# Weight halves and sums laid out in DRAM in parts of 2,048 bytes a partition

## The chip, the cores and the metric

The kernel runs on one core of one Trainium2 chip. The metric is device time in microseconds (us), from the start of the program to its end. All times below are of the whole program, and the trace is of one profiled execution.

## The reference

Eight batches of attention with a softmax over the feature axis of q and over the sequence axis of k, then a gated feed-forward network over all 4,608 tokens:

```
q_s = softmax(q, last axis); k_s = softmax(k, sequence axis)
kv  = einsum('bhsd,bhse->bhde', k_s, v)            # 8 batches, 8 heads, 576 x 64
x   = einsum('bhsd,bhde->bhse', q_s, kv)  -> (4608, 512)
xn  = x / sqrt(mean(x*x) + 1e-6) * rms_g
out = (silu(xn @ w_gate) * (xn @ w_val)) @ w_out   # 512 -> 1536 -> 512
```

All inputs and outputs are float32.

## The kernel before

The 4,608 tokens are nine blocks of 512. Each float32 product is made of three TensorE products of a high and a low half (`float32r`), so every weight is held as a pair of halves. The first three blocks run plainly: `f1` multiplies the normalised tokens by a tile of gate and value weights, `f2` multiplies the gated result by a tile of output weights; a step number s counts 12 tiles per block. The other six blocks are three pairs. A pair goes through a Strassen scheme: seven products (`pp`, numbered 1 to 7) of sums of weight quarters with sums of token blocks take the place of eight, for each of six tile pairs i and two column groups m. The last two pairs do the same for the output weights (`qq`).

The halves are made once, in block 1 (`w_hi`, `w_lo`, `o_hi`, `o_lo`), and kept in DRAM: `w_keep` (line 940) writes the four parts of a weight tile, `s_keep` (line 981) the sums of weights that the Strassen products need, `o_keep` (line 944) the halves of the output weights. They go to tensors `wd` (one for each of six tile pairs) and `od` (one for each of 12 tiles). These writes are issued from SyncE (SP). They are read back from GpSimd's queue (POOL): `w_back` (line 948) and `o_back` (line 952) for block 2, `w_in` (line 1118) and `o_in` (line 1130) for the pairs. A `w_in` brings part 1 (four parts: S2, S1, A11, A12; 1,024 KB) or part 2 (three parts: A22, S3, S4; 768 KB) of one m into a slot of a ring; there are four slots, and a slot is loaded again right behind the last product that reads it.

An explicit list, `ORDER`, gives the order in which the steps are written, and so the order on each engine and each queue; a letter behind a step (A, D, P) names the engine for it. POOL also computes: it makes low halves (`h_lo`, line 1017; `hp_lo`, line 1220), token sums (`t_add`, line 1089) and parts of the softmax of q. Between the plain blocks and the pairs, at about 340 to 380 us, block 2's last tiles, the first token sums of pair 0 and the attention of blocks 5 and 6 stand side by side. `q_load` (line 670) brings a q tile from DRAM in pieces of 128-byte runs through SP's queue; `q_max` (line 736) on VectorE (DVE) is the first to read it.

The layout before, and the reads and writes that use it, are these lines:

```
wd = [tc.dram_tile([2, P, 8, 2, HALF], F32, ...)]       # m, partition, part, half, 256
od = [tc.dram_tile([P, 2, DM], F32, ...)]
parts_of(i, at, n): wd[i][:, :, at:at + n] -> "m p a b f -> p m a (b f)"
w_in: src = wd[i][m, :, :4] if part == 1 else wd[i][m, :, 5:]     # one run a partition
```

Of the kernel before, what the change touches and what calls it, by code (L numbers as in the profile page):

```python
# [8 lines left out]
F32 = mybir.dt.float32  # L9
I32 = mybir.dt.int32  # L10
U32 = mybir.dt.uint32
F32R = mybir.dt.float32r
# [337 lines left out]
def linear_attention_then_gated_ffn(ctx: ExitStack, tc, q, k, v, w_gate, w_val, w_out, rms_g, out):  # L350
    nc = tc.nc
    B, H, S, D = q.shape
    NT, DM = out.shape
    DF = w_gate.shape[1]
    P = 128
    NG = H // 2
    NKT = DM // P
    NF = DF // P
# [14 lines left out]
    NH = NF // 2  # L373
    HALF = TB // 2
    assert NB == JP + 2 * NPAIR and NKT == 4 and NF == 2 * NH

    wsp = ctx.enter_context(tc.tile_pool(name="wsp", bufs=2))
# [28 lines left out]
    def on(default):  # L406
        return unit[0] or default
# [488 lines left out]
    wh_, wo_, h_, po, g_, v_ = {}, {}, {}, {}, {}, {}  # L896
    ov = out.rearrange("(j t p) m -> j t p m", p=P, t=T)
    ov0 = out.rearrange("(j p t) m -> j t p m", p=P, t=T)

    def w_tile(s):  # L900
        if s not in wh_:
            wh_[s] = wsp.tile([P, 2, 2, 2, HALF], F32R, name="w")
        return wh_[s]

    def o_tile(s):
# [9 lines left out]
    def w_hi(s, a, n):  # L915
        copy(w_tile(s)[:, a:a + n, :, 0], halves(s % NF, a, n), nc.scalar)

    def w_lo(s, a):
        w = w_tile(s)[:, a]
        on(nc.gpsimd).tensor_tensor(out=w[:, :, 1], in0=halves(s % NF, a, 1)[:, 0], in1=w[:, :, 0].bitcast(F32),  # L920
                                    op=ALU.subtract)
# [6 lines left out]
        on(nc.vector).tensor_tensor(out=ol, in0=W(s % NF, 2), in1=oh.bitcast(F32), op=ALU.subtract)  # L928

    S2, S1, A11, A12, A21, A22, S3, S4 = range(8)  # L930
    wd = [tc.dram_tile([2, P, 8, 2, HALF], F32, name=f"wd{i}") for i in range(NH)]
    od = [tc.dram_tile([P, 2, DM], F32, name=f"od{i}") for i in range(NF)]
    ot_ = {}

    def parts_of(i, at, n):
        return wd[i][:, :, at:at + n].rearrange("m p a b f -> p m a (b f)")

    def w_keep(s):
        i, odd = divmod(s % NF, 2)
        on(nc.sync).dma_start(parts_of(i, A21 if odd else A11, 2),  # L940
                          wh_[s].rearrange("p m a b f -> p m a (b f)").bitcast(F32))

    def o_keep(s):
        on(nc.sync).dma_start(od[s % NF], ot_[s].bitcast(F32))

    def w_back(s):
        i, odd = divmod(s % NF, 2)
        nc.gpsimd.dma_start(w_tile(s).rearrange("p m a b f -> p m a (b f)"), parts_of(i, A21 if odd else A11, 2))

    def o_back(s):  # L950
        o = wsp.tile([P, 2, DM], F32R, name="o")
# [26 lines left out]
        on(nc.gpsimd).tensor_tensor(out=t[:, :, 1], in0=f, in1=t[:, :, 0].bitcast(F32), op=ALU.subtract)  # L978

    def s_keep(i, n):  # L980
        on(nc.sync).dma_start(parts_of(i, {1: S1, 2: S2, 3: S3, 4: S4}[n], 1)[:, :, 0],
                          split[i, n].rearrange("p m b f -> p m (b f)").bitcast(F32))

    done = {}
# [57 lines left out]
    XF, XO, RING, WO, H2, TMP, HH = {}, {}, {}, [], {}, {}, {}  # L1042
# [61 lines left out]
    def ring():  # L1104
        if not RING:
            t0 = big.tile([P, 6, TB], F32R, name="ring_0", tag="raw_0")
            t1 = big.tile([P, 6, TB], F32R, name="ring_1", tag="raw_1")
            RING[1] = [t0[:, :4]]
            RING[2] = [t1[:, :3], t1[:, 3:]]
            WO.append(t0[:, 4:])  # L1110

    def w_in(p, i, m, part):
        ring()
        if part == 1 and m == len(RING[1]):
            RING[1].append(wsp.tile([P, 4, TB], F32R, name="w"))
        t = RING[part][m].rearrange("p a b -> p (a b)")
        src = wd[i][m, :, :4] if part == 1 else wd[i][m, :, 5:]
        nc.gpsimd.dma_start(t, src.rearrange("p a b f -> p (a b f)"))  # L1118

    def o_in(p, t, c):  # L1120
        ring()
# [309 lines left out]
    def e_put(x, h):  # L1431
# [7 lines left out]
              n_t, n_y0, n_y1, o_hi, o_lo, q_c0, q_eps0, q_exp, q_half, q_half2, q_hi, q_lo, q_load, q_load0, q_max,  # L1439
              q_max0, q_max2, q_mul, q_mul0, q_rec, q_rec0, q_sub, q_sub0, q_sum, q_sum0, q_sum2, q_t, q_t0, q_x, q_x0,  # L1440
              silu, store, w_keep, o_keep, w_back, o_back, s_add, s_hi, s_lo, s_keep, x_cp, x_nm, t_add, b_hi, b_lo,
              w_in, o_in, r_keep, r_load, t_sum, t_hi, t_lo, t_keep, qw, q_t1, q_t2, q_t3, q_t4, qb_hi, qb_lo, qq, qs1, qu2, qu3,
              q22, q21, q12, qtr, qput, qpua, pp, c_s1, c_u2, c_u3, c_11, c_21, c_22, c_12, gate, hm, e_add, e_tr, e_copy, e_put, hp_hi, hp_lo, f2p, put, v_load, v_ones, w_hi, w_lo, warm, x_acc, x_hi, x_lo, x_sq)}

# [33 lines left out]
```

## Time and profile before

| what | value |
|---|---|
| runs | 943.98, 944.52, 946.81 us |
| median | 944.52 us |
| profiled execution, its own time | 944.05 us |
| its span, first to last instruction | 941.8 us |
| TensorE (PE) busy | 924.7 us, 98% of the span |
| PE weight loads busy | 748.9 us |
| VectorE (DVE) busy | 729.5 us, 77% |
| ScalarE (ACT) busy | 467.4 us, 50% |
| GpSimd (POOL) busy | 532.8 us, 57% |
| DMA packets, all queues | 210,298 for 212.65 MB |
| POOL's DMA queue (q0) | 16,320 packets, 88.09 MB |
| SP's DMA queue (q1) | 187,568 packets, 122.86 MB |

An engine's busy time divided by the span is its share; PE's is near the whole, so its idle times, and what ended them, are what there is to win. "PE" rows are matmuls, "PEld" rows the loads of the stationary operand. The two DMA queues share 16 DMA engines; a packet of the trace is one run of bytes.

### The profile page before, as it was taken

To read this page: it belongs to the slowest core of one execution; us is meant where nothing else is said; L and a number is where in the kernel's file an instruction comes from. 1 tells how busy PE (TensorE), PEld (TensorE's weight loads), DVE (VectorE), ACT (ScalarE), POOL (GpSimd) and SP (SyncE) were. 2 spreads that over 40 slices of the span, in tenths; PEclk is the share of its full clock that TensorE was granted. 3 is DMA by queue.
4 is the path that set the end of the run, shared out by engine and by line. 5 is a ranking of instruction groups with operands and counts; after the bars stand their busy time and mean duration, and the time that the engine had idled before them with its cause. 6 is when DMAs were issued, how large, how long until landed. Compare 5 with 4: busy or idle time off the path is not lost.

```text
span 941.8 us, 14336 instructions
## 1 busy us (share of the span) xinstructions
PE 924.7 (98%) x4621; PEld 748.9 (80%) x4621; DVE 729.5 (77%) x1526; ACT 467.4 (50%) x748; POOL 532.8 (57%) x546
## 2 busy tenths in 40 slices
PE   8999999999999998999999999999999999999998
PEld 6687877887877886888888888888888888888886
DVE  6989879988978996877877788775458975646586
ACT  4998848765678764655644364322215522111241
POOL 4887978877677995667764535433532423332403
PEclk9999999999999999999999999999999999999999
DMA  9997528989977999798995699888665778855255
GB/s 237 285 249 227 157 47 283 295 269 311 289 247 210 240 249 239 192 254 223 254 248 181 198 286 282 279 292 296 187 210 176 218 193 264 271 203 179 66 158 90
DMA packets 210298, 212.65 MB, mean 226 GB/s; under 512 B 132144, under 2 KB 171568, under 8 KB 205616
## 3 DMA queue, kind: packets, MB, share of 16 engines
q1 hardware_dynamic: 187568, 122.86, 47.7%
q0 software_dynamic: 16320, 88.09, 29.9%
q10 hardware_dynamic: 6336, 0.79, 0.6%
q8 instruction: 37, 0.61, 0.3%
q14 instruction: 37, 0.30, 0.1%
HBM read 161.35 MB, written 50.33 MB: 225 GB/s over the span
## 4 chain that ended last, share of the span: by engine, by line
PE 83%; DMA 7%; DVE 3%; ACT 2%; issue 2%; SPq 2%; POOL 0%; DVEq 0%; ACTq 0%
PE ps_gv L1145 18%; PE ps_gv L996 14%; PE ps_o L1145 12%; PE ps_o L1033 7%; PE ps_a L1145 7%; PE ps_o L1354 6%; PE ps_o L1238 4%; PE ps_a L1354 4%; PE ps_gv L1354 3%; DMA qt<-in_q_dram 2%; PE ps_a L1238 2%; PE ps_gv L1238 2%; DMA w<-in_v_dram 2%; PE ps_a L600 2%; PE ps_a L808 2%
## 5 line engine op out<-in xcount | busy, mean ns | idle before, releaser
L996 PE MATMUL ps_gv<-xh,w 128*128 128x512 f32 x576 | 191.8, 399 | 1.1 <-DVE gs L1008 1.1
L1145 PE MATMUL ps_gv<-x,ring 128*128 128x512 f32 x576 | 143.0, 392 | 0.0
L996 PEld LDWEIGHTS ps_gv<-xh,w 128*128 128x128 f32 x576 | 108.5, 188 | 26.9 <-DVE gs L1008 2.1
L1145 PEld LDWEIGHTS ps_gv<-x,ring 128*128 128x128 f32 x576 | 107.0, 188 | 23.0
L996 PE MATMUL ps_gv<-xl,w 128*128 128x512 f32 x288 | 112.6, 392 | 0.0
L1166 DVE TENSOR_TENSOR tmp<-tmp,ps_gv 128x512 f32<-128x512 f32 x84 | 57.3, 684 | 49.5 <-PE ps_gv L1145 47.8
L1145 PE MATMUL ps_o<-x,ring 128*128 128x512 f32 x360 | 85.1, 389 | 0.0
L1118 POOL DMA_DIRECT2D ring<-wd x54 | 31.0, 575 | 91.2 <-PE ps_o L1145 34.1
L1145 PEld LDWEIGHTS ps_o<-x,ring 128*128 128x128 f32 x360 | 67.6, 188 | 14.2
L1033 PE MATMUL ps_o<-o,hh 128*128 128x512 f32 x288 | 73.5, 396 | 0.0
L996 PEld LDWEIGHTS ps_gv<-xl,w 128*128 128x128 f32 x288 | 54.5, 189 | 10.7 <-issue 0.4
L1033 PEld LDWEIGHTS ps_o<-o,hh 128*128 128x128 f32 x288 | 52.9, 188 | 11.8 <-ACT ot L416 0.7
L1166 DVE TENSOR_TENSOR tmp<-tmp,ps_o 128x512 f32<-128x512 f32 x42 | 28.7, 685 | 29.1 <-PE ps_o L1145 25.7
L920 POOL TENSOR_TENSOR w<-w,w 128x512 fp32r<-128x512 f32 x34 | 45.9, 1359 | 8.2 <-ACT w L411 7.6
L411 ACT CAST hh<-gs 128x512 fp32r<-128x512 f32 x48 | 29.6, 617 | 30.4 <-DVE gs L1008 16.0
L1033 PE MATMUL ps_o<-o,hl 128*128 128x512 f32 x144 | 39.7, 399 | 4.3 <-DVE hl L1017 4.3
L1118 POOL DMA_DIRECT2D w<-wd x18 | 10.1, 559 | 58.0 <-PE ps_a L1145 37.8
L547 DVE TENSOR_REDUCE cm<-kt 128x128 f32<-128x640 f32 x28 | 36.7, 1312 | 3.1 <-DMA kt<-in_k_dram 3.0
L1145 PE MATMUL ps_a<-x,w 128*128 128x512 f32 x144 | 36.9, 392 | 0.0
L1017 POOL TENSOR_TENSOR hl<-gs,hh 128x512 fp32r<-128x512 f32 x21 | 28.1, 1339 | 15.2 <-DMA qt<-in_q_dram 6.0
L1145 PE MATMUL ps_a<-x,ring 128*128 128x512 f32 x144 | 36.7, 390 | 0.0
L1033 PEld LDWEIGHTS ps_o<-o,hl 128*128 128x128 f32 x144 | 27.4, 191 | 10.9 <-DVE hl L1017 4.7
(632 smaller groups left out, 2320.3 us busy)
## 6 DMA issues: line engine op xcount, KB each, us to landing
ring<-wd POOLq DMA_DIRECT2D x36, 768.0 KB, 5.6
w<-wd POOLq DMA_DIRECT2D x24, 1024.0 KB, 6.0
ring<-wd POOLq DMA_DIRECT2D x18, 1024.0 KB, 5.7
wd<-w SPq DMA_DIRECT2D x12, 1024.0 KB, 5.2
wd<-parts SPq DMA_DIRECT2D x24, 512.0 KB, 3.6
o<-od POOLq DMA_DIRECT2D x18, 512.0 KB, 5.7
od<-o SPq DMA_DIRECT2D x12, 512.0 KB, 3.8
out_dram<-ot SPq DMA_DIRECT2D x20, 256.0 KB, 4.2
```

Source lines behind the costliest of these rows:

```text
L411: (e.copy if e is nc.scalar else e.tensor_copy)(dst, src)
L547: nc.vector.tensor_reduce(out=cm, in_=kt_[b, g].rearrange("p h j d -> p h d j"), axis=AX.X, op=ALU.max)
L600: nc.tensor.matmul(pk[h * D:(h + 1) * D, :D + 1], lhsT=ke[:, h, j], rhs=vt[:, j, h], start=(j == 0), stop=(j == CH - 1))
L920: on(nc.gpsimd).tensor_tensor(out=w[:, :, 1], in0=halves(s % NF, a, 1)[:, 0], in1=w[:, :, 0].bitcast(F32), op=ALU.subtract)
L996: nc.tensor.matmul(pd[s], lhsT=w[:, a, c // 2, m, c % 2 * P:c % 2 * P + P], rhs=X[j, c][x], start=(n == 1), stop=(n == 3 * NKT))
L1017: on(nc.gpsimd).tensor_tensor(out=hl, in0=g_[s], in1=h_[s][0].bitcast(F32), op=ALU.subtract)
L1033: nc.tensor.matmul(po[t], lhsT=a[:, t * P:(t + 1) * P], rhs=w, start=(i == 0 and n == 0), stop=(i == NF - 1 and n == len(terms) - 1))
L1118: nc.gpsimd.dma_start(t, src.rearrange("p a b f -> p (a b f)"))
L1145: nc.tensor.matmul(abc[p, i, m, b], lhsT=src[:, h, c * P:(c + 1) * P], rhs=operand(o, c, x), start=first and n == 0, stop=n == 5, skip_gro ...
L1166: nc.vector.tensor_tensor(out=dst, in0=ux[u + (src,)], in1=abc[u + (b,)], op=ALU.add)
L1238: nc.tensor.matmul(pa[p, t, k], lhsT=a[:, k * P:(k + 1) * P], rhs=w, start=(c == 0 and n == 0), stop=(c == NF - 1 and n == 2))
L1354: nc.tensor.matmul(qacc[p, b, x], lhsT=ws[l][x], rhs=h[m], start=first and i == 0 and n == 0, stop=i == NH - 1 and n == 2, skip_group_chec ...
```

## The change

The parts of `wd` now lie one behind the other, each as 128 partitions of 2,048 bytes, with the part number outermost; `od` likewise has its two halves outermost. So a partition's data for a load are no longer one run of 8,192 or 6,144 bytes (`w_in`), two runs of 4,096 (`w_back`) or one of 4,096 (`o_back`, `o_in`), but four, three, four or two runs of 2,048. Writes: `w_keep` goes from two runs of 4,096 bytes a partition to four of 2,048, `o_keep` from one of 4,096 to two of 2,048; `s_keep` had two of 2,048 and has them still. To keep one order on both sides, the weight tile in SBUF is ordered by part and then by m (`wt_`), and `wh_` is a view of it in the old order of indices. The bytes moved, the number of DMAs and the place of every instruction on its engine stay as they were.

```diff
+    wt_ = {}
+
     def w_tile(s):
         if s not in wh_:
-            wh_[s] = wsp.tile([P, 2, 2, 2, HALF], F32R, name="w")
+            wt_[s] = wsp.tile([P, 4, 2 * HALF], F32R, name="w")
+            wh_[s] = wt_[s].rearrange("p (k m) (b f) -> p m k b f", k=2, b=2)
         return wh_[s]
...
-    wd = [tc.dram_tile([2, P, 8, 2, HALF], F32, name=f"wd{i}") for i in range(NH)]
-    od = [tc.dram_tile([P, 2, DM], F32, name=f"od{i}") for i in range(NF)]
+    wd = [tc.dram_tile([8, 2, P, 2 * HALF], F32, name=f"wd{i}") for i in range(NH)]
+    od = [tc.dram_tile([2, P, DM], F32, name=f"od{i}").rearrange("m p f -> p m f") for i in range(NF)]
...
     def parts_of(i, at, n):
-        return wd[i][:, :, at:at + n].rearrange("m p a b f -> p m a (b f)")
+        return wd[i][at:at + n].rearrange("k m p f -> p (k m) f")
 
     def w_keep(s):
         i, odd = divmod(s % NF, 2)
-        on(nc.sync).dma_start(parts_of(i, A21 if odd else A11, 2),
-                          wh_[s].rearrange("p m a b f -> p m a (b f)").bitcast(F32))
+        on(nc.sync).dma_start(parts_of(i, A21 if odd else A11, 2), wt_[s].bitcast(F32))
...
     def w_back(s):
         i, odd = divmod(s % NF, 2)
-        nc.gpsimd.dma_start(w_tile(s).rearrange("p m a b f -> p m a (b f)"), parts_of(i, A21 if odd else A11, 2))
+        w_tile(s)
+        nc.gpsimd.dma_start(wt_[s], parts_of(i, A21 if odd else A11, 2))
...
-        on(nc.sync).dma_start(parts_of(i, {1: S1, 2: S2, 3: S3, 4: S4}[n], 1)[:, :, 0],
+        on(nc.sync).dma_start(parts_of(i, {1: S1, 2: S2, 3: S3, 4: S4}[n], 1),
                           split[i, n].rearrange("p m b f -> p m (b f)").bitcast(F32))
...
-        t = RING[part][m].rearrange("p a b -> p (a b)")
-        src = wd[i][m, :, :4] if part == 1 else wd[i][m, :, 5:]
-        nc.gpsimd.dma_start(t, src.rearrange("p a b f -> p (a b f)"))
+        src = wd[i][:4, m] if part == 1 else wd[i][5:, m]
+        nc.gpsimd.dma_start(RING[part][m], src.rearrange("k p f -> p k f"))
```

On POOL, at the passage from block 2 to pair 0 (about 356 to 362 us), these are the rows before: the last `w_back` (line 948), two `w_in` (line 1118), a token sum in two steps (line 1089), an `o_back` and an `o_in`. The figures behind a DMA are partitions by runs by elements of 4 bytes.

```order
-L948 DMA w<-wd_109 128x2x1024
-L1118 DMA ring_3742<-wd_104 128x2048
-L1089 TENSOR_TENSOR xl<-xl 128x512
-L1089 TENSOR_TENSOR ot<-xl,xh 128x512
-L1118 DMA ring_3743<-wd_104 128x1536
-L952 DMA o<-od_120 128x1024
-L1130 DMA x_4251<-od_111 128x1024
```

And these are the same rows after the change, in the same order; only the shapes of the DMAs differ (and the line numbers, by two or three).

```order
+L951 DMA w<-wd_109 128x4x512
+L1120 DMA ring_3742<-wd_104 128x4x512
+L1092 TENSOR_TENSOR xl<-xl 128x512
+L1092 TENSOR_TENSOR ot<-xl,xh 128x512
+L1120 DMA ring_3743<-wd_104 128x3x512
+L955 DMA o<-od_120 128x2x512
+L1132 DMA x_4251<-od_111 128x2x512
```

## Rows read from the trace of the kernel before

**Rows 1.** Busy time by stretch, PE alone: start and end, length, busy, clock, DMA share, GB/s.

```profile
330.00:380.00 50.00, 45.73 (x234) 0.97 0.99 229
...
605.00:720.00 115.00, 115.00 (x508) 1.00 0.75 241
```

**Rows 2.** What PE waited for, whole span: us in total, times, longest.

```profile
PE ps_o L1033 <- DVE hl L1017: 4.3, 1, 4.3
PE ps_a L573 <- DVE kx L568: 3.6, 3, 2.3
```

**Rows 3.** Timeline, 360 to 371 us: start, us, engine, line, operation, [idle before <-releaser].

```profile
360.99 0.62 ACT L411 CAST hh<-gs 128x512 fp32r<-128x512 f32 x1
...
364.08 1.97 PE L1033 MATMUL ps_o<-o,hh 128*128 128x512 f32 x8
...
366.80 0.69 DVE L736 TENSOR_REDUCE st<-qt 128x16 f32<-128x512 f32 x1 [7.05 <-issue]
...
369.58 0.68 DVE L1017 TENSOR_TENSOR hl<-gs,hh 128x512 fp32r<-128x512 f32 x1
...
370.32 2.07 PE L1033 MATMUL ps_o<-o,hl 128*128 128x512 f32 x4 [4.26 <-DVE hl L1017]
```

**Rows 4.** DMA issues of 357.73 to 357.75 us: KB each, us to landing.

```profile
qt<-in_q_dram SPq DMA_DIRECT2D x1, 16.0 KB, 8.8
```

**Rows 5.** DMA issues of 268 to 284 us, where POOL's queue is empty.

```profile
qt<-in_q_dram SPq DMA_DIRECT2D x16, 32.0 KB, 2.0
```

**Rows 6.** DMA queues, 358 to 360 us: packets, MB, share of 16 engines.

```profile
q0 software_dynamic: 124, 0.51, 100.0%
```

**Rows 7.** DMA queues, 362 to 364 us.

```profile
q0 software_dynamic: 96, 0.73, 94.5%
q1 hardware_dynamic: 133, 0.04, 32.9%
```

**Rows 8.** Chain that ended last, 368 to 380 us: start, us, what.

```profile
372.61 3.35 PE ps_gv L996 x12
...
376.86 2.75 PE ps_gv L996 x12
```

**Rows 9.** Busy time by stretch, 370.32 to 375.94 us: PE, PEld, DVE, ACT, POOL, clock, DMA.

```profile
370.32:375.94 5.62, 5.62 (x19) 4.44 (x20) 5.37 (x18) 4.81 (x9) 4.30 (x4) 0.70 0.68 112
```

**Rows 10.** POOL's groups by line: busy us, mean ns | idle before, releasers.

```profile
L1118 POOL DMA_DIRECT2D w<-wd x18 | 10.1, 559 | 58.0 <-PE ps_a L1145 37.8 <-PE ps_o L1145 20.2
...
L948 POOL DMA_DIRECT2D w<-wd x6 | 4.7, 783 | 4.6 <-PE ps_gv L996 4.3 <-issue 0.3
```

**Rows 11.** Timeline of POOL and PEld, 387 to 419 us.

```profile
387.83 1.29 POOL L1017 TENSOR_TENSOR hl<-gs,hh 128x512 fp32r<-128x512 f32 x1
...
389.67 0.87 PEld L1033 LDWEIGHTS ps_o<-o,hl 128*128 128x128 f32 x4
...
402.16 1.30 POOL L1017 TENSOR_TENSOR hl<-gs,hh 128x512 fp32r<-128x512 f32 x1
403.99 0.64 PEld L1033 LDWEIGHTS ps_o<-o,hl 128*128 128x128 f32 x3
```

**Rows 12.** POOL's timeline, 356 to 362 us.

```profile
356.55 0.77 POOL L948 DMA_DIRECT2D w<-wd  x1 [2.40 <-PE ps_gv L996]
357.31 0.55 POOL L1118 DMA_DIRECT2D ring<-wd  x1
...
359.13 1.30 POOL L1089 TENSOR_TENSOR ot<-xl,xh 128x512 f32<-128x512 f32 x1
```

**Rows 13.** DMA issues, whole span: KB each, median us to landing.

```profile
w<-wd POOLq DMA_DIRECT2D x24, 1024.0 KB, 6.0
...
wd<-parts SPq DMA_DIRECT2D x24, 512.0 KB, 3.6
```

**Rows 14.** The chain, 639 us: seven products of one i and m.

```profile
639.31 9.52 PE ps_o L1145 x42
```

## Prediction

> **What bounds the kernel now.** I read the busy time by stretch first. PE is busy 115.00 of 115.00 us in the stretch from 605 us on, and so it is through nearly all of the pairs; the one poor stretch after the start is 330 to 380 us, with 45.73 of 50.00 and a granted clock of 0.97 [rows 1]. The list of PE's waits gives the reasons: no entry names a load from `wd` or `od`, and the largest is a single wait of 4.3 us for a low half made by DVE [rows 2]. So a faster or slower `wd` load is worth nothing by itself; what counts is what these loads do to others, and there the timeline of 360 to 371 us is the place to look [rows 3]. DVE stands idle for 7.05 us before `q_max` (L736), which reads a q tile. Behind it, in order, comes the low half `hl` that PE's output product needs. PE ends its products with the high half at 364.08 + 1.97 = 366.05 us, waits 4.26 us, and goes on at 370.32.
>
> Why the q tile is late is in the DMA views. Its last piece, 16 KB, was issued at 357.73 us and took 8.8 us to land [rows 4]; where POOL's queue moves nothing, pieces twice that size land in 2.0 us [rows 5]. From 358 to 360 us the 16 DMA engines moved 124 packets of POOL's queue q0 and none of SP's q1 [rows 6]. From 362 to 364 us both moved: 96 packets of q0 with 0.73 MB, so 7.6 KB each, and 133 of q1 with 0.04 MB [rows 7]. That is about one small packet for one big one, and the big one takes nearly all of the time. The piece of 16 KB is 128 runs of 128 bytes, 8 for each engine, and each waits behind a run of up to 8 KB.
>
> **The change part by part.** The weight reads of `w_in` come in runs of 2 KB where they had 8 or 6; `w_back` and the loads from `od` had 4. If the queues take turns packet by packet, as [rows 7] has it, the same 0.73 MB would be some 356 packets in 2 us, and q1 would be served about four times as often. Then the 128 runs need about 0.5 us and not some 2 to 4. What the change cannot shorten is the first part of the delay, in which q1 moved nothing [rows 6]. I put the landing at 363.0 us, between 359.7 (2.0 us after the issue, as in [rows 5]) and 366.5 (as now). From the start of `q_max` to the end of `hl` DVE needs 369.58 + 0.68 - 366.80 = 3.46 us [rows 3], so `hl` would be ready at 366.5, and of PE's wait 0.5 us would be left: **-3.8 us**. The bounds are 0 (q1 is served as before) and -4.3 (landing by 362.5).
>
> After the wait the granted clock is 0.70 in 370.32 to 375.94 us [rows 9], between the levels of 2.4 and 1.2 GHz, behind an idle PE. The four `hl` products take 2.07 us there, where eight of the same shape took 1.97, so 1.0 is lost [rows 3]; the next 12 products take 3.35 against 2.75 for the 12 after them, 0.6 more [rows 8]. With no more than 0.5 us of idling I take this as saved: **-1.6 us**, bounds 0 and -1.6.
>
> On the other side POOL spends longer on issuing. A load of one run a partition takes 559 ns, one of two runs 783 ns [rows 10], so 0.22 us for each further run: four runs 1.22 us, three 1.00. No row shows four; the bounds are 0.78 (no growth past two runs) and 2.24 (four times 559 ns), and I take 1.22, since the only step that a row shows is 0.22. Over 36 loads of four runs, 36 of three, 6 `w_back` (two to four) and 30 from `od` (one to two) it is 36 x 0.66 + 36 x 0.44 + 6 x 0.44 + 30 x 0.22 = 49 us of POOL's time, which is idle for 409 us. On the path is only what POOL makes for PE right behind a load. In pair 0 `hl` follows a `w_in` and ends at 389.12 and 403.46 us, and PE loads it at 389.67 and 403.99 [rows 11]: margins of 0.55 and 0.53. A load longer by 0.66 takes 0.11 and 0.13 out of PE, and I allow for two more such places: **+0.3 us**. With loads of 2.24 it would be four times 1.68 - 0.55, or +4.5; with loads of 0.78, 0.
>
> At 356 to 362 us POOL issues a `w_back` and a `w_in`, then the token sum that ends at 360.43 [rows 12]. With 0.44 + 0.66 more it ends at 361.5. ACT casts the sum and then the high half, now at 360.99 to 361.61 [rows 3]; that moves to about 362.7, still before PE wants it at 364.08. Cost: nothing, while loads stay below about 1.8 us each.
>
> The loads themselves may land later. Between the reload of a ring slot and its next use lie at least the seven products of the other m, 9.52 us [rows 14], and loads of 1,024 KB land in 6.0 [rows 13]: 3.5 us are spare, so nothing. Writes: `s_keep` writes runs of 2 KB now and lands 512 KB in 3.6 us, a `w_keep` of twice the size is not on PE's list of waits, so nothing. The view of the weight tile changes what ACT's casts step over, not their size; PE waits for no ACT entry, so nothing either.
>
> The sum, against the profiled execution's own 944.05 us, which is 0.47 below the median of the runs: 944.05 - 3.8 - 1.6 + 0.3 = 938.95, **939.0 us**. About 0.3% (2.8 us) is what a measurement of this kernel can tell from no change, so "same" is 941.7 to 947.4.
>
> **The rivals.** *The queues take longer turns.* For: [rows 6] shows 2 us of `w_back` with no q1 packet between. If each load with several runs a partition goes as one turn, all loads now behave like `w_back`; the last q piece waits out one further load of 1 MB and lands near 365.0, which leaves 2.5 us of the wait, and perhaps half of the clock's loss: 944.05 - 1.8 - 0.8 + 0.3 = 941.8. The Trainium skill has this rule (DMA: Bandwidth & Descriptors, section on queues, rings and completion order): an engine drains a whole packet of one queue, some 9 to 17 runs, before it turns to the other. By that rule it comes to the 941.8; rows 6 agree with it and rows 7, with nearly equal counts, rather do not.
>
> *Nothing moves*: q1 is late for a reason of its own queue, such as slow issue, and the 4.26 us stay. Against it stands the 2.0 us of [rows 5]. With POOL's 0.3 it gives 944.4.
>
> *POOL pays in full proportion*: 938.95 - 0.3 + 4.5 = 943.2.
>
> *POOL holds, the slower case.* If it can have only so many runs outstanding, it stops in front of a load until the one before has landed. The rows show no stop with a `w_back` of 256 runs and a `w_in` of 128 within 0.76 us [rows 12]; the change makes them 512 and 512. If the `w_in` of 357.31 must wait for the `w_back` to land (6.0 us after 356.55, so 362.6), the token sum comes 5.3 us later, the high half is ready at about 366.9 and PE loses 2.8 us there; the loads behind it hold POOL for about 6 us again, with the first sums of pair 0 behind them, so that PE's first product comes later by as much. It decides as soon as two such loads do not fit together: 944.05 - 4.3 + 2.8 + 6.0 = 948.6. The Trainium skill (same page, section on terms) says that such a load's descriptors, of 16 bytes each, are kept in rings in SBUF. The kernel reserves 1,024 bytes a partition for them, and an estimate from that page's figure is 64 for each engine, where two loads of 512 runs make 64 without their ends: by that estimate the hold would be real but short, as room comes free run by run, and the sum stays at 939.0 within 1 us.
>
> **How the numbers follow.** The forecast has 0.50, with a range of its own of 937.5 to 941.5 from the bounds of its terms. Longer turns have 0.20 (940.5 to 943.5), nothing 0.10, proportion 0.08, the hold 0.12. The range of 937.0 to 946.5 leaves out the hold and a little below. Faster: nearly all of 0.50 and a little under half of 0.20, so 0.57; slower: 0.12, the hold; same: the remaining 0.31.
>
> **What would show it.** q0's packets rise from 16,320 to about 44,700, since the loads have 36 x 512 + 36 x 384 + 6 x 512 + 30 x 256 = 43,008 runs where they had 14,592. `q_max` at about 360 us shows an idle time below 4 us in place of 7.05, PE's wait for `hl` shrinks below 1 us and the clock stays at 1.00 there. POOL's loads of four runs last about 1.2 us, and small waits of PE for POOL's `hl` appear near 389 and 404 us. The prediction is wrong if the q piece still takes over 7 us, if POOL's loads take 2 us or more, or if a long idle time appears on POOL in front of a load with nothing to wait for.

## The result, and the profile after

The change takes 954.45 us (median of six runs, 949.55 to 960.51) against 943.66 us of the kernel before beside it (six runs, 938.82 to 946.81): a ratio of 1.0123, 95% interval 1.0076 to 1.0170. It is slower, by some 11 us. The forecast was 939.0 us. The rival that came true is "POOL holds", which had a chance of 0.12 and lay outside the range; at 948.6 us it stood 4.5 us above the kernel before, so it too was priced at less than half. The ratios here and below leave out executions that took over 1.5% more than the fastest of the same kernel, as 2 of the 35 of the kernel before beside experiments 1 and 2 did, and 4 of the 17 beside 3 to 5.

The profiled execution took 956.03 us, its span is 953.9. These are the page's busy times and the two queues, then two rows of the view by stretch (columns as in [rows 9]):

```profile
PE 928.4 (97%) x4621; PEld 749.9 (79%) x4621; DVE 733.0 (77%) x1526; ACT 466.6 (49%) x748; POOL 555.8 (58%) x546
...
q1 hardware_dynamic: 192176, 122.86, 47.5%
q0 software_dynamic: 44736, 88.09, 34.1%
```

```profile
330.00:380.00 50.00, 45.12 (x229) 36.33 (x228) 39.08 (x101) 28.22 (x43) 38.26 (x42) 0.97 1.19 254
...
605.00:720.00 115.00, 115.00 (x508) 94.90 (x506) 73.67 (x126) 25.76 (x45) 47.54 (x46) 1.00 0.86 254
```

q0 has 44,736 packets, as forecast (about 44,700), for the same 88.09 MB. PE is still full from 605 us on; 330 to 380 us is no better than in [rows 1]. PE's list of waits has changed, though. The 4.3 us for DVE's low half [rows 2] are gone, and in their place stands a wait of nearly the same size for a high half made by ACT:

```profile
PE ps_a L573 <- DVE kx L568: 4.6, 3, 3.3
PE ps_o L1036 <- ACT hh L411: 3.9, 1, 3.9
...
PE ps_a L1240 <- POOL hl L1222: 1.6, 1, 1.6
```

ACT's row says what it waited for (the timeline, 372 to 374 us):

```profile
372.17 0.62 ACT L411 CAST x<-ot 128x512 fp32r<-128x512 f32 x1 [8.01 <-POOL ot L1092]
372.70 0.61 ACT L411 CAST hh<-gs 128x512 fp32r<-128x512 f32 x1
373.36 3.68 PE L1036 MATMUL ps_o<-o,hh 128*128 128x512 f32 x8 [3.86 <-ACT hh L411]
```

ACT stood 8.01 us for the token sum, and the high half is next in its order. POOL made that sum late, and its own timeline, the counterpart of [rows 12], shows why:

```profile
361.76 0.81 POOL L951 DMA_DIRECT2D w<-wd  x1 [1.78 <-PE ps_gv L999]
368.89 0.75 POOL L1120 DMA_DIRECT2D ring<-wd  x1 [6.32 <-issue]
369.65 1.27 POOL L1092 TENSOR_TENSOR xl<-xl 128x512 f32<-128x512 f32 x1
370.88 1.26 POOL L1092 TENSOR_TENSOR ot<-xl,xh 128x512 f32<-128x512 f32 x1
372.08 0.78 POOL L1120 DMA_DIRECT2D ring<-wd  x1
375.00 0.74 POOL L955 DMA_DIRECT2D o<-od  x1 [2.14 <-issue]
```

Before, the `w_in` followed the `w_back` at once. Now POOL stands 6.32 us in front of it, and 2.14 us in front of the `o_back`, with nothing in the view for it to wait for ("issue"). The view of DMA issues gives the end of the stop. The `w_back` of 361.76 took 6.8 us to land:

```profile
w<-wd POOLq DMA_DIRECT2D x1, 1024.0 KB, 6.8
```

So it landed at 361.76 + 6.8 = 368.56, and the held load began 0.33 us behind that. Issues in front of which POOL idled for "issue" by over 0.3 us add up to 17.9 us over the span; in the kernel before there was none.

I then set, for each of POOL's 108 loads, its runs (128 partitions by the runs of a partition) beside those of the loads issued and not yet landed. In the profile of the change the sum reaches 896 and never 1,024: no two loads of 512 runs are ever outstanding together. Thirteen loads in front of which POOL stood idle for over 0.3 us, and which would have brought the sum to 1,024 or more before the last landing, begin 0.31 to 0.34 us behind that landing. Six of them are the ones that the view puts down to "issue", with the 17.9 us; for the other seven it names a semaphore of another engine or a DMA, so how much of their idle time is a hold is not shown. In the kernel before the sum reaches 768. That gave the theory for the runs below: **room theory**, POOL stops in front of a load until its descriptors fit into the 1,024 bytes a partition that the program reserves (`dynamic_dma_scratch_size`), so that fewer than 1,024 runs are ever outstanding, and room comes back when a load has landed.

### The profile page after: what moved, and what is told of

The parts are those of the page before. It is cut to its first block, busy times and chain, and to the rows that moved or that the text cites. A ratio compares the mean times of both kernels' runs of the same rounds, so it can differ in the third digit from the quotient of the medians.

```text
span 953.9 us, 14336 instructions
## 1 busy us (share of the span) xinstructions
PE 928.4 (97%) x4621; PEld 749.9 (79%) x4621; DVE 733.0 (77%) x1526; ACT 466.6 (49%) x748; POOL 555.8 (58%) x546
## 3 DMA queue, kind: packets, MB, share of 16 engines
q0 software_dynamic: 44736, 88.09, 34.1%
## 4 chain that ended last, share of the span: by engine, by line
PE 74%; DMA 8%; POOL 5%; DVE 4%; issue 4%; SPq 2%; ACT 1%; POOLq 0%; ACTq 0%; DVEq 0%
PE ps_gv L1147 15%; PE ps_o L1147 12%; PE ps_gv L999 12%; PE ps_o L1036 6%; PE ps_o L1356 6%; PE ps_a L1147 6%; PE ps_a L1356 3%; PE ps_o L1240 3%; DMA qt<-in_q_dram 3%; PE ps_gv L1356 3%; DMA raw<-in_moe_w_gate_dram 2%; DMA vt<-in_v_dram 2%; PE ps_a L1240 2%; PE ps_a L600 1%; PE ps_gv L1240 1%
## 5 line engine op out<-in xcount | busy, mean ns | idle before, releaser
L1120 POOL DMA_DIRECT2D ring<-wd x54 | 42.6, 790 | 91.4 <-PE ps_o L1147 34.0
L1120 POOL DMA_DIRECT2D w<-wd x18 | 14.3, 795 | 55.5 <-PE ps_a L1147 31.0
L1147 PE MATMUL ps_gv<-x,w 128*128 128x512 f32 x144 | 35.1, 391 | 0.0
```

The lines of the kernel that those rows point to most:

```text
L1120: nc.gpsimd.dma_start(RING[part][m], src.rearrange("k p f -> p k f"))
L1147: nc.tensor.matmul(abc[p, i, m, b], lhsT=src[:, h, c * P:(c + 1) * P], rhs=operand(o, c, x), start=first and n == 0, stop=n == 5, skip_gro ...
```

## The experiments

**1. More room, and nothing else.** Both kernels with 2,048 bytes for descriptors, and the change taken apart. All four (e1 to e4) ran on one chip; the kernel before has a median of 945.13 us there (35 runs).

```diff
-    nc = _bacc.Bacc("TRN2", ..., dynamic_dma_scratch_size=1024)
+    nc = _bacc.Bacc("TRN2", ..., dynamic_dma_scratch_size=2048)     # e1: in the change; e2: in the kernel before
```

> The changed kernel with 2,048 bytes a partition reserved for descriptors in place of 1,024; nothing else differs. Theory H (POOL may have only so many runs outstanding, and with 512 runs a load it stops until an earlier load has landed): the idle times before loads on POOL that end on nothing visible (6.32 us before the ring load at 368.89 us, 3.35 before 584.15, 3.02 before 515.96, 2.14 before 375.00) go, PE's wait of 3.9 us for ACT's hh and the 1.6 us for POOL's hl go with them, and the time falls by some 4 to 10 us from the changed kernel's 954 to between 944 and 950; the q piece at the passage then shows whether finer runs serve q1 sooner (if so below 943). Theory W (the writes or the loads in runs of 2 KB are slower in themselves, or q1 is served worse): the holds may go, but the time stays within 3 us of 954.

> The kernel before with 2,048 bytes a partition reserved for descriptors: control for the first run. Both theories: no hold is seen in the trace of the kernel before (no idle time on POOL before a load of over 0.3 us that ends on nothing visible), so the time stays within 0.3% of 943.7. If it falls as well, the reserve helps for another reason and the first run's gain cannot be put down to the runs.

With room, the change takes 945.25 us (12 runs), ratio to the kernel before 1.0012 [0.9982, 1.0042]. The loss is gone as far as the interval tells, and all holds with it. The time is not below 943 us either, which was to be the sign that finer runs serve the q tile sooner. POOL's timeline:

```profile
357.92 0.81 POOL L951 DMA_DIRECT2D w<-wd  x1 [1.97 <-PE ps_gv L999]
358.72 0.75 POOL L1120 DMA_DIRECT2D ring<-wd  x1
359.48 1.31 POOL L1092 TENSOR_TENSOR xl<-xl 128x512 f32<-128x512 f32 x1
```

The `w_in` goes out right behind the `w_back`, with the same runs and the same traffic. The kernel before gains nothing by the room: 943.65 us, 0.9993 [0.9955, 1.0030].

**2. One of the two layouts alone.** `wd` in parts with the old `od` (e3), and the reverse (e4), with 1,024 bytes.

```diff
-    wd = [tc.dram_tile([2, P, 8, 2, HALF], F32, ...)]
+    wd = [tc.dram_tile([8, 2, P, 2 * HALF], F32, ...)]              # e3: this alone, with its reads and writes
-    od = [tc.dram_tile([P, 2, DM], F32, ...)]
+    od = [tc.dram_tile([2, P, DM], F32, ...).rearrange("m p f -> p m f")]    # e4: this alone
```

> Only the weight tensors wd in parts of 2,048 bytes; od as before (one run of 4,096 bytes a partition). Theory H: the pair of w_back and w_in of 512 runs each still does not fit, so the hold of about 6 us stays and most of the loss with it: 950 to 955. Where two od loads follow (375 and 584 us) the holds shrink. Theory W: as much of the loss as the wd traffic has of the bytes, 950 to 954.

> Only od in two halves of 2,048 bytes a partition; wd as before. Theory H: loads of at most 256 runs, no hold of over 1 us, time within 0.3% of 943.7. Theory W: a small loss, 1 to 3 us.

`wd` alone gives 952.54 us, 1.0095 [1.0062, 1.0129]; `od` alone 944.09 us, 1.0012 [0.9971, 1.0053]. The loss is `wd`'s. In its profile the same load is held, for 6.17 us, and PE waits as in the change:

```profile
369.73 0.74 POOL L1120 DMA_DIRECT2D ring<-wd  x1 [6.17 <-issue]
```

```profile
PE ps_o L1036 <- ACT hh L411: 3.8, 1, 3.8
```

Of the two holds in front of loads from `od` that were to shrink in e3, the one of 584 us is gone and the one of 375 us is not smaller (2.56 us). In e4 one hold is left, where a load of 256 runs would have brought the sum to 1,024; it begins 0.31 us behind a landing:

```profile
363.79 0.72 POOL L1130 DMA_DIRECT2D x<-od  x1 [0.72 <-issue]
```

**3. Twice the runs in twice the room.** This asks whether the limit goes by runs, or whether 2,048 bytes are just enough for anything. Parts of 1,024 bytes: eight, six and eight runs a partition. The weight tile, the reads and the writes follow the new parts (not shown).

```diff
-    wd = [tc.dram_tile([8, 2, P, 2 * HALF], F32, ...)]
+    wd = [tc.dram_tile([8, 2, 2, P, HALF], F32, ...)]
...
-    nc = _bacc.Bacc("TRN2", ..., dynamic_dma_scratch_size=1024)
+    nc = _bacc.Bacc("TRN2", ..., dynamic_dma_scratch_size=2048)
```

> The change with parts of 1,024 bytes in wd (eight, six, eight runs a partition in place of four, three, four) and 2,048 bytes of room for descriptors in place of 1,024. Room theory, counted in runs: twice the runs in twice the room is the same case as the change, so the holds of POOL come back: 10 to 18 us in all (a little less, since the od loads keep two runs and now need half as much of the room), one of 4 to 7 us before the w_in at about 369 us, and the time is 949 to 957 us, against 945 without the halving. Rival, the room only has to be above some fixed size for loads of this number and these bytes: no holds, 943 to 948 us. On the issue: if its price goes by the runs, a load of eight runs takes over 1.0 us; if it is flat from two runs on, 0.75 to 0.85.

The holds are back, 21.5 us of them, and the time is 964.15 us, 1.0199 [1.0131, 1.0268], above what I had expected. The runs outstanding never pass 1,792, twice 896. The load behind the `w_back` is held again, to its landing 8.7 us after 368.55, and 0.3 more:

```profile
368.55 0.95 POOL L951 DMA_DIRECT2D w<-wd  x1 [1.02 <-PE ps_gv L1000]
377.57 0.88 POOL L1121 DMA_DIRECT2D ring<-wd  x1 [8.07 <-issue]
```

```profile
w<-wd POOLq DMA_DIRECT2D x1, 1024.0 KB, 8.7
```

That the time passes the expected 957 has two visible parts: this hold is longer, as the loads land later, and the stretch with the writes, 190 to 300 us, took 117.3 us where it takes 109.9 to 112.3 in every other profile (the table below).

**4. The same runs in more loads.** Each `w_in` as two DMAs.

```diff
-        nc.gpsimd.dma_start(RING[part][m], src.rearrange("k p f -> p k f"))
+        t, n = RING[part][m], 2
+        nc.gpsimd.dma_start(t[:, :n], src[:n].rearrange("k p f -> p k f"))
+        nc.gpsimd.dma_start(t[:, n:], src[n:].rearrange("k p f -> p k f"))
```

> The change with 1,024 bytes of room as it was, and each w_in issued as two DMAs behind each other (two runs and two, or two and one). Room theory, counted in runs: the sum of runs is the same, so the room is full at the same point: holds of 10 to 18 us in all, now before the second half at the passage, the token sum as late as before (PE waits 3 to 4.5 us for the high half), and 950 to 957 us with some 72 more issues of 0.78 us on POOL. Rival, one load of 512 runs is too large beside another, whatever the sum is: halves of 256 runs go through at once as in the kernel before, holds under 2 us, 943 to 948 us. Second rival, a limit on the number of loads: more loads, more holds, over 25 us.

951.94 us, 1.0071 [1.0030, 1.0111]. The first half goes out beside the `w_back`, and the second is held to the `w_back`'s landing, at 359.69 + 6.4 = 366.1:

```profile
359.69 0.81 POOL L951 DMA_DIRECT2D w<-wd  x1 [1.73 <-PE ps_gv L999]
360.56 0.71 POOL L1121 DMA_DIRECT2D ring<-wd  x1
366.44 0.71 POOL L1122 DMA_DIRECT2D ring<-wd  x1 [5.17 <-issue]
```

```profile
w<-wd POOLq DMA_DIRECT2D x1, 1024.0 KB, 6.4
```

So it is neither the size of one load nor the number of loads, but the sum of runs, which reaches 896 here too. The holds came to 9.0 us, a little below the expected 10 to 18. I take this to be so because half a load fits earlier than a whole one; it was not tested.

**5. Another order at the passage.** The first `w_in` behind the token sum.

```diff
-h_mul.33 w_in.0.0.0.1 q_max.6.1 ...
+h_mul.33 q_max.6.1 ...
-... t_add.0.1.0:P f1.34.0 ...
+... t_add.0.1.0:P w_in.0.0.0.1 f1.34.0 ...
```

> The change, with the one w_in of the passage (part 1 of m 0, the load behind the last w_back) moved behind the token sum that followed it. Room theory with the cost by what stands behind the held load: the hold stays (2 to 6 us, less what the token sum takes), the other holds too, but PE's wait of 3.9 us for the high half goes to under 0.7 us unless the wait for DVE's low half takes its place; the time is 1 to 4 us below the change, 950 to 953.5 us. Rival, the loss does not come from what stands behind the load but from late loads or from the traffic: no difference from the change within 0.3%, 953 to 956 us.

955.54 us, 1.0109 [1.0046, 1.0171]: no gain over the change (1.0123) that these six runs show, so the expected 950 to 953.5 was missed. The wait for the high half is gone as foreseen, but the holds have only moved, to one of 3.81 us behind the sum and one of 5.36 in front of the `o_back`:

```profile
362.35 1.29 POOL L1092 TENSOR_TENSOR ot<-xl,xh 128x512 f32<-128x512 f32 x1
367.45 1.53 POOL L1120 DMA_DIRECT2D ring<-wd  x2 [3.81 <-issue]
374.35 0.73 POOL L955 DMA_DIRECT2D o<-od  x1 [5.36 <-issue]
```

PE now waits 1.6 us at 371 us for DVE's low half, and 1.5 us at 387 us, in pair 0, for an operand (`x`). That these waits are the price of the moved holds is likely but not shown; moving one load did not make the loss smaller.

**6. The wait that the prediction wanted to remove.** Single executions of the two layouts with 1,024 or 2,048 bytes, for DVE's idle time at `q_max` and PE's wait for the low half.

> The kernel before, unchanged, for a second profile. Theory that the wait on which the prediction rested was one execution's: DVE's idle time before q_max at about 360 us is under 5 us, and PE's wait for the low half of DVE under 2 us, as in the two profiles in which the layout of wd was the old one. Rival, it is steady: 6.5 to 7.5 us and 4 to 4.6 us.

> The kernel before, unchanged, once more, since the look before this one came out at over twice every other time, with each product of 128 x 512 at 0.83 us, and tells nothing of the wait. Theory that the wait on which the prediction rested was one execution's: DVE's idle time before q_max at about 360 us is under 5 us, and PE's wait for the low half of DVE under 2 us. Rival, it is steady: 6.5 to 7.5 us and 4 to 4.6 us.

> The change with 2,048 bytes of room, unchanged, for a second look at the q tile. Theory that finer runs serve the q tile sooner: PE's wait for DVE's low half at about 365 us is under 0.7 us here too, as in the first look (none), and the span is 937 to 944 us. Rival, the wait comes and goes by execution whatever the runs are: over 1.5 us in one of the two looks. No holds of POOL in either theory.

> As for the look before, a third look at the change with room: under 0.7 us of PE's wait for DVE's low half by the theory of finer runs, over 1.5 us in one of the two by the rival.

> The kernel before with 2,048 bytes of room, a second look. By the theory of finer runs the wait for DVE's low half can be long here, as in two of the four looks at the old layout (4.3 and 8.9 us, against 0.2 and none): 0 to 9 us, and its size decides the span. By the rival, the same spread as with the new layout.

e8 tells nothing of this: that execution took 2,248.8 us, every product of 128 x 512 some 0.83 us, for a reason that no view shows. The others took 952.19 (e9), 946.81 (e10), 951.71 (e11) and 942.51 us (e12), one execution each and on other chips, so the times are not compared here. PE's waits for DVE's low half, from e9, then e10, e11 and e12:

```profile
PE ps_o L1033 <- DVE hl L1017: 8.9, 1, 8.9
```

```profile
PE ps_o L1036 <- DVE hl L1020: 5.6, 2, 4.8
```

```profile
PE ps_o L1036 <- DVE hl L1020: 5.4, 2, 4.7
```

```profile
PE ps_o L1033 <- DVE hl L1017: 3.6, 1, 3.6
```

So with the old layout of `wd` the wait at the passage is 4.3 [rows 2], 8.9, 3.6, 0.2 (e2) and 0 us (e4); with the new one and room it is 4.8, 4.7 and 0 (e1). Both theories fell. The wait is not one execution's accident, since five of eight profiles have 3.6 us or more of it; and finer runs do not take it away. What goes with it is the order of issue. In e4 the last q piece of 16 KB was issued at 357.83 us, 0.13 before the `w_back`, and took 1.9 us; in e10 four such pieces were issued at 359.57 to 361.36, behind a `w_back` of 358.69, and took 6.9 (median). The other six profiles agree, though no run moved a q piece alone: in e1 the last piece was issued between the `w_back` and the `w_in`, took 4.1 us, and PE did not wait; in the five others at least one was issued behind both loads, and the last took 5.1 (e2) to 11.2 us (e9). This is so although the queues took turns as the prediction had it (the DMA view of e4 at 357.8 us, then of e10 for 360 to 362 us and, the two queues, for 362 to 364):

```profile
qt<-in_q_dram SPq DMA_DIRECT2D x1, 16.0 KB, 1.9
```

```profile
qt<-in_q_dram SPq DMA_DIRECT2D x4, 16.0 KB, 6.9
```

```profile
q0 software_dynamic: 348, 0.71, 116.7%
q1 hardware_dynamic: 322, 0.04, 46.0%
```

Where [rows 7] had 96 packets of q0 and 133 of q1 in 2 us, there are now 348 and 322: about one for one as before, and q1 served 2.4 times as often in packets, though with 0.04 MB both times. The tile was still late; five q pieces stood behind the `w_back` of e10, where the kernel before had two.

**Where the 11 us are.** I took the time between the starts of the same products of PE in each profile, with the stretches cut at the products that begin at 190, 300, 330, 400 and 605 us in the kernel before (us; 300 to 330 took 30.1 in all of them, and the rest from 605 on 336.7 or 336.8):

| profiles | to 190 | 190 to 300 | 330 to 400 | 400 to 605 | span |
|---|---|---|---|---|---|
| old `wd` (before, e2, e4, e9, e12), mean | 191.1 | 110.2 | 68.6 | 205.6 | 942.4 |
| new `wd`, 2,048 bytes (e1, e10, e11), mean | 190.5 | 111.8 | 68.5 | 206.5 | 944.3 |
| the change | 192.1 | 112.1 | 71.2 | 211.6 | 953.9 |
| e3, `wd` alone | 192.9 | 112.3 | 71.0 | 209.0 | 952.0 |

Against the mean of the old layout the change loses 1.0, 1.9, 2.6 and 6.0 us. With room the 2.6 and most of the 6.0 are absent, but one or a few profiles of a kernel do not show that the holds make them. At the passage the old `wd` alone ranges from 63.8 to 74.6, so 2.6 is within what executions differ by: PE's wait behind the hold has taken the place of the one behind the q tile. In pair 0 the change lies above every profile with the old `wd` (204.9 to 206.7) or with room (205.2 to 208.0), and seven of the 13 held loads are there. PE idles for 5.1 us in that stretch. Of these 2.6 stand at 466 to 469 us, behind DVE's wait for a q tile, and e11, which has no holds, idles for 2.2 at the same products; the largest wait of each is this (the change, then e11):

```profile
PE ps_gv L1147 <- DVE tmp L1168: 1.8, 1, 1.8
```

```profile
PE ps_gv L1147 <- DVE tmp L1168: 1.4, 1, 1.4
```

PE's wait of 1.6 us for a low half, shown above, is behind a held load (the change, 584 to 587 us; e3, whose `od` loads have one run a partition, has no such wait):

```profile
584.15 0.74 POOL L1132 DMA_DIRECT2D x<-od  x1 [3.35 <-issue]
584.91 2.52 POOL L1222 TENSOR_TENSOR hl<-xl,hh 128x512 fp32r<-128x512 f32 x2
...
586.24 0.50 PE L1240 MATMUL ps_a<-o,hl 128*128 128x512 f32 x1 [1.60 <-POOL hl L1222]
```

That the holds cost the whole is thus shown by the runs with room (1.0123 against 1.0012), not by this table, and how the loss divides over the stretches stays open. Of the 1.9 in the stretch with the writes 1.6 are there with room as well; it is the one cost of finer runs by themselves that the profiles hint at, and I did not test what makes it.

## Why the prediction was wrong

*The step that failed* is the last sentence of the rival "POOL holds": that "the hold would be real but short, as room comes free run by run, and the sum stays at 939.0 within 1 us". The rival's own mechanism was right to the instruction. The `w_in` behind the `w_back` waits until that has landed, 6.32 us where 5.3 were worked out, and PE loses 3.86 where 2.8 were. Room comes free by whole loads here: each of the 13 held loads began 0.31 to 0.34 us behind the landing of an earlier one. The size of the rival was off in its other term: the 6.0 us in front of PE's first product of pair 0 did not come (PE waits for nothing from 377 to 410 us), while holds later in pair 0, which the rival did not have, go with a loss there. The prediction even had the number in hand. The Trainium skill (DMA: Bandwidth & Descriptors, section Terms) gives 16 bytes for a descriptor; by an estimate from this, 1,024 bytes make 64 an engine, or 1,024 runs over 16 engines, and two loads of 512 runs do not fit once anything more is needed for a load. The runs agree: the outstanding sum stays at 896, and at twice the room at 1,792 or, in e1, 1,920. That sum alone should have put the hold among the likely cases. What made me put it at 0.12 was a guess about how room is given back, for which I had no row.

The forecast would have failed without the hold too: with room, and no hold, the ratio is 1.0012 [0.9982, 1.0042] where the forecast, 5.1 us less than before, is 0.995. What failed there is the next term.

*-3.8 us, the q tile*: failed. That q1 is served more often is right (322 packets for 133), that the tile then lands in time is not: q pieces behind a `w_back` took 6.9 us with the new layout too. In the change itself the last two, issued at 363.00 and 363.36 us behind the `w_back` of 361.76, landed at 368.77 and 368.97, and DVE stood idle for 3.91 us before `q_max`, which began 0.27 us behind the last of them (the view names another DMA). For 364 to 365 us the view of the queues names q0 alone, with runs of 2,048 bytes as [rows 6] had it with longer ones:

```profile
q0 software_dynamic: 175, 0.36, 114.1%
```

```profile
369.24 0.69 DVE L736 TENSOR_REDUCE st<-qt 128x16 f32<-128x512 f32 x1 [3.91 <-DMA vt<-in_v_dram]
```

So the tile was late here as well, and PE's wait for it is hidden by the longer one for the high half. Nearly equal counts of packets, from which the prediction read turns of one run, could come of longer turns too, so the rival of longer turns is not ruled out. The price was right: in e1, e2 and e4, where PE waits for DVE's low half by 0.2 us or less, the passage takes 64.2, 65.1 and 63.8 us, 4.9 to 6.2 less than the 70.0 of the kernel before, and the prediction's two terms make 5.4. But e2 and e4 have the old `wd`: it is not the layout that takes the wait away.

*-1.6 us, the clock*: it hung on the same wait. In the change the products behind the new wait of 3.86 us take 3.68 us for eight, where [rows 3] have 1.97, the granted clock in these 3.68 us is 0.54, and that of 330 to 380 us is 0.97 as before; so the clock's loss has moved with the wait.

*+0.3 us, POOL's issuing*: the size was off, on the safe side. Four runs take 0.79 us, not 1.22:

```profile
L1120 POOL DMA_DIRECT2D ring<-wd x54 | 42.6, 790 | 91.4 <-PE ps_o L1147 34.0 <-PE ps_a L1147 27.5 <-PE ps_gv L1147 15.7
...
L1120 POOL DMA_DIRECT2D w<-wd x18 | 14.3, 795 | 55.5 <-PE ps_a L1147 31.0 <-PE ps_o L1147 19.4 <-PE ps_gv L1147 5.1
...
L951 POOL DMA_DIRECT2D w<-wd x6 | 4.9, 824 | 2.1 <-PE ps_gv L999 1.8 <-issue 0.3
```

This is the lower bound that the prediction named, no growth past two runs [rows 10]; POOL's busy time rose by 23 us, not 49. The Trainium skill has it so (same page, section "Anatomy of one DMA — SWDGE (gpsimd) path"): "You can emit a lot of descriptors before the incremental cost shows up". Here the cost of a `w_back` goes from 783 ns at two runs to 824 at four and 958 at eight (e5), between the two values that were expected for eight.

*"Cost: nothing, while loads stay below about 1.8 us each"* at 356 to 362 us: the loads stayed at 0.8 us, and PE waited at the passage all the same, because what grew was not the issue but the time in front of it.

*Loads landing later, writes, casts, nothing*: holds for the loads, whose median for 1,024 KB went from 6.0 [rows 13] to 6.9 us without an entry in PE's list. For the writes it may be off by 1.6 to 1.9 us, as said. No cast grew.

*The end of the range*: "a long idle time ... on POOL in front of a load with nothing to wait for" was named as the sign that the prediction is wrong, and it is the one that came.

## What to carry to other kernels

Count the runs of all loads that are outstanding on GpSimd's queue at once, not only the bytes and the issue time (in these runs they stayed below 1,024 with 1,024 bytes a partition reserved, and below 2,048 with 2,048): cutting runs to a quarter of their length gave loads that cost 0.79 us to issue and still stopped the engine for 6 us, because two of them no longer fitted. A stop in front of a DMA that the profile puts down to "issue" and that ends some 0.3 us behind the landing of an earlier load was this here; more room took it away without any other edit. And before a wait in one profile is made a term of the sum, look at whether it depends on a race between two queues: here it was 0 to 8.9 us in five profiles with the same `wd`.

## What was not expected of the hardware

Room came back with the landing of a load: each of the 13 held loads of the change began 0.31 to 0.34 us behind a landing, and so did the six of e5, with 2,048 bytes. The issue of a load costs 0.56 us at one run a partition (`w_in` before) and, for a `w_back`, 0.78 at two, 0.82 at four and 0.96 at eight, so 0.02 to 0.03 us for a further run. And a small transfer issued behind a `w_back` took nearly as long with the new layout (6.9 us in e10) as with the old one (8.8, [rows 4]), though its queue was served more than twice as often in packets; whether that is the longer list of transfers in front of it on its own queue, I did not test.
